# GroupNorm over a ring of six tiles: stores and loads in runs of four, last stores in quarters, one tile summed on TensorE alone

## The chip, the cores and the metric

The kernel runs on one core of one Trainium2 chip. The metric is device time in microseconds (us), as a median over executions. The kernel before takes 632.62 us (632.31 to 633.0 in the four runs beside the changed kernel). Two kernels are compared only on the same chip; runs are set side by side by their ratios to the kernel before. Each trace quoted is of a single execution.

## The reference

```python
# x: bf16 (128, 1024, 32, 16), g and b: bf16 (1024)
G = 32
xr = x.reshape(B, G, C // G, H, W)
mu = xr.mean(axis=(2, 3, 4), keepdims=True)
var = ((xr - mu) ** 2).mean(axis=(2, 3, 4), keepdims=True)
xn = ((xr - mu) / jnp.sqrt(var + 1e-5)).reshape(B, C, H, W)
return xn * g[None, :, None, None] + b[None, :, None, None]
```

A group is 32 channels of 512 elements, 16,384 in all. Four images of 32 groups fill the 128 partitions, so the work is 32 tiles of 128 x 16,384 bf16, 4.19 MB each. Each must be loaded once and stored once: 268.4 MB.

## The kernel before

A ring in SBUF, the on-chip memory, holds six tiles; a tile is normalised in place. SP, the engine that here only waits and issues, starts all large DMA transfers on one queue (the page of before: 32 loads and 35 stores, 268.44 MB, all on q1), in the order of its program, and waits for semaphores between them. In the traces the transfers land in the order of their issue.

```python
SLOTS = 6
RUNS = (2, 3, 3, 3, 3, 3, 3, 3, 3, 6)
NQ = 4
PE_CHUNKS = 12          # of 32 chunks of 512 elements; the other 20 are summed on VectorE

def store_parts(i):
    return NQ if i == NT - 1 else 1

def on_sync(e):
    def load(j):
        if j >= SLOTS:
            e.wait_ge(st[j % SLOTS], 16 * (j // SLOTS))      # the slot's store has landed
        e.dma_start(out=slot(j), in_=x_v[j]).then_inc(ld[j % SLOTS], 16)
    def store(i):
        w = F // store_parts(i)
        for p in range(store_parts(i)):
            e.wait_ge(done, NQ * i + NQ // store_parts(i) * (p + 1))   # VectorE has scaled it
            e.dma_start(...)                                            # cut
    for j in range(SLOTS):
        load(j)
    i = 0
    for run in RUNS:
        for n in range(run):
            store(i + n)
        i += run
        for j in range(i + SLOTS - run, min(i + SLOTS, NT)):
            load(j)
```

For each tile, TensorE adds 12 chunks into a PSUM buffer with an identity matrix, VectorE adds the rest in one pairing instruction, ScalarE makes the mean and then two passes of squares with the mean as bias, and VectorE scales the tile in 32 instructions.

```python
# TensorE, tile in slot c of round t
for k in range(PE_CHUNKS):
    ...                                              # waits, cut
    elif k == PE_CHUNKS - 1:
        e.wait_ge(paired, t * SLOTS + (c + 1))
    mm = e.matmul(out=sums(c), lhsT=eye[:], rhs=slot(c)[:, k * MM_FREE : (k + 1) * MM_FREE], ...)

# VectorE
pair(0)
with nc.Fori(0, NT, 1, engines=[e.engine]) as i:
    with e.If(i < NT - 1):
        e.drain()
        pair(i + 1)              # waits until TensorE has begun tile i + 1, so until it is loaded
    ...                          # wait for the deviation; scale and bias; 32 scalings; done += 1 per quarter
```

Of the kernel before, what the change touches and what calls it, by code (L numbers as in the profile page):

```python
# [14 lines left out]
EPS = 1e-5  # L15

SLOTS = 6
RUNS = (2, 3, 3, 3, 3, 3, 3, 3, 3, 6)
NQ = 4
PS_BUFS = 3  # L20
PE_CHUNKS = 12
MM_FREE = 512
# [3 lines left out]
def kernel(  # L26
# [13 lines left out]
    nc = tc.nc  # L40
# [7 lines left out]
    NT = B0 // NS  # L48
    KC = C // G
    F = KC * HW  # L50
    inv_n = 1.0 / float(F)
    NMM = F // MM_FREE
    ROUNDS = -(-NT // SLOTS)
    REST = NT - (ROUNDS - 1) * SLOTS
    KQ = KC // NQ
    PAIRED = F - PE_CHUNKS * MM_FREE
    ITEM = 2
    assert NT > SLOTS and 0 < REST < SLOTS and sum(RUNS) == NT and RUNS[-1] == SLOTS
    assert F % MM_FREE == 0 and PAIRED % 2 == 0 and SLOTS % PS_BUFS == 0
# [6 lines left out]
    def sbuf(name, shape, dtype):  # L66
        return nc.alloc_sbuf_tensor(name, shape, dtype)


    ring = sbuf("ring", [P, SLOTS * F], BF16)  # L70
# [4 lines left out]
    eye = sbuf("eye", [P, P], BF16)  # L75
# [13 lines left out]
    ps = nc.alloc_psum_tensor("ps", [P, PS_BUFS * 2 * MM_FREE], F32)  # L89
    gb_p = nc.alloc_psum_tensor("gb_p", [P, 2 * KC], F32)  # L90

    def sem(name):
        return nc.alloc_semaphore(name)
# [8 lines left out]
    first_in, paired, stded, done = (sem(n) for n in ("first", "pair", "std", "done"))  # L102
# [2 lines left out]
    )  # L105

    def store_parts(i):
        return NQ if i == NT - 1 else 1

    def slot(i):  # L110
        return ring[:, (i % SLOTS) * F : (i % SLOTS + 1) * F]

    def sums(c):
        return ps[:, c % PS_BUFS * 2 * MM_FREE : c % PS_BUFS * 2 * MM_FREE + MM_FREE]

    def sums_and_pairs(c):
        return ps[:, c % PS_BUFS * 2 * MM_FREE : c % PS_BUFS * 2 * MM_FREE + MM_FREE + 1]

    def on_sync(e):
        def load(j):  # L120
            if j >= SLOTS:
                e.wait_ge(st[j % SLOTS], 16 * (j // SLOTS))
# [5 lines that stand above are left out]
                e.wait_ge(done, NQ * i + NQ // store_parts(i) * (p + 1))  # L128
                e.dma_start(
                    out=o_v[i][:, p * w : (p + 1) * w], in_=slot(i)[:, p * w : (p + 1) * w]  # L130
                ).then_inc(st[i % SLOTS] if i + SLOTS < NT else s_fin, 16)
# [10 lines that stand above are left out]
        e.wait_ge(s_fin, 16 * sum(store_parts(i) for i in range(NT - SLOTS, NT)))  # L142
# [19 lines left out]
    def in_rounds(e, one):  # L162
        with nc.Fori(0, ROUNDS, 1, engines=[e.engine]) as t:
            for c in range(REST):
                one(c, t)
            with e.If(t < ROUNDS - 1):
                for c in range(REST, SLOTS):
                    one(c, t)

    def on_tensor(e):  # L170
        e.wait_ge(s_eye, 2)
        e.wait_ge(s_gb, 32)
        e.matmul(out=gb_p[:], lhsT=rep[:], rhs=gb_b[:], start=True, stop=True).then_inc(s_gbp, 1)  # L173

        def one(c, t):
            for k in range(PE_CHUNKS):
                if k == 0:
                    e.wait_ge(ld[c], (t + 1) * 16)
                elif k == PE_CHUNKS - 2:

                    e.wait_ge(meaned[(c - 2) % SLOTS], t + 1)
                elif k == PE_CHUNKS - 1:
                    e.wait_ge(paired, t * SLOTS + (c + 1))
                mm = e.matmul(  # L184
                    out=sums(c),
                    lhsT=eye[:],
                    rhs=slot(c)[:, k * MM_FREE : (k + 1) * MM_FREE],
                    start=(k == 0),
                    stop=(k == PE_CHUNKS - 1),
                )  # L190
                if k == 0:
                    mm.then_inc(first_in, 1)
            mm.then_inc(summed[c], 1)

        in_rounds(e, one)

    def on_scalar(e):
# [5 lines left out]
        def one(c, t):  # L203
            e.wait_ge(summed[c], t + 1)
            e.activation(  # L205
                out=jm[:], in_=sums_and_pairs(c), func=ACT.Identity, scale=-inv_n,
                accum_out=nm[:, c : c + 1], saturate=False,
            ).then_inc(meaned[c], 1)
            for h, (ready, at) in enumerate(
                ((meaned[c], t + (2 if c >= SLOTS - 2 else 1)), (half[c], t + 1))  # L210
            ):
                e.wait_ge(ready, at)
                e.activation(  # L213
                    out=ja[:],
                    in_=slot(c)[:, h * (F // 2) : (h + 1) * (F // 2)],
                    func=ACT.Square,
                    bias=nm[:, c : c + 1],
                    scale=1.0,
                    accum_out=sq[:, h : h + 1],
                    saturate=False,  # L220
                ).then_inc((half, both)[h][c], 1)
            e.wait_ge(both[c], t + 1)
            e.activation(  # L223
                out=var[:], in_=sq[:, 0:1], func=ACT.Identity, bias=eps_t[:], scale=inv_n
            ).then_inc(varred[c], 1)
            e.wait_ge(varred[c], t + 1)
            e.activation(  # L227
                out=std[:, c : c + 1], in_=sq[:, 1:2], func=ACT.Sqrt, bias=var[:], scale=inv_n
            ).then_inc(stded, 1)
# [3 lines left out]
    def on_vector(e):  # L233
        bytes_of_ring = ring[:].bitcast(mybir.dt.uint8)

        def part(i, lo, n):
            at = (i % SLOTS) * (F * ITEM) + lo * ITEM
            return bytes_of_ring[:, bass.ds(at, n * ITEM)].bitcast(BF16)

        def pair(i):  # L240
            lo, n = PE_CHUNKS * MM_FREE, PAIRED // 2
            e.wait_ge(first_in, i + 1)
            e.scalar_tensor_tensor(  # L243
                out=jp[:],
                in0=part(i, lo, n),
                scalar=1.0,
                in1=part(i, lo + n, n),
                op0=ALU.mult,
                op1=ALU.add,
                accum_out=ps[:, bass.ds((i % PS_BUFS) * (2 * MM_FREE) + MM_FREE, 1)],  # L250
                saturate=False,
            ).then_inc(paired, 1)

        e.wait_ge(s_gbp, 1)
        e.tensor_copy(out=gb[:], in_=gb_p[:])  # L255
        pair(0)
        with nc.Fori(0, NT, 1, engines=[e.engine]) as i:
            with e.If(i < NT - 1):
                e.drain()  # L259
                pair(i + 1)  # L260
            parts = [part(i, k * HW, HW) for k in range(KC)]
            e.keepalive_nop([e.lower_ap(a) for a in parts])  # L262
            e.wait_ge(stded, i + 1)
            e.reciprocal(out=rstd[:], in_=std[:, bass.ds(i % SLOTS, 1)]).then_inc(inverted, 1)  # L264
            e.wait_ge(inverted, i + 1)
            e.tensor_scalar(  # L266
                out=scl[:], in0=gb[:, 0:KC], scalar1=rstd[:], scalar2=None, op0=ALU.mult
            ).then_inc(scaled, 1)
            e.wait_ge(scaled, i + 1)
            e.scalar_tensor_tensor(  # L270
                out=bia[:], in0=scl[:], scalar=nm[:, bass.ds(i % SLOTS, 1)],
                in1=gb[:, KC : 2 * KC], op0=ALU.mult, op1=ALU.add,
            ).then_inc(shifted, 1)
            e.wait_ge(shifted, i + 1)
            for k, a in enumerate(parts):
                ts = e.tensor_scalar(  # L276
                    out=a, in0=a, scalar1=scl[:, k : k + 1], scalar2=bia[:, k : k + 1],
                    op0=ALU.mult, op1=ALU.add,
                )
                if (k + 1) % KQ == 0:  # L280
                    ts.then_inc(done, 1)

    with tc.tile_critical(no_gpsimd_drain=True):  # L283
        on_sync(nc.sync)
        on_gpsimd(nc.gpsimd)
        on_tensor(nc.tensor)
        on_scalar(nc.scalar)
        on_vector(nc.vector)
# [30 lines left out]
```

## Time and profile before

| | before |
|---|---|
| median | 632.62 us |
| profiled span | 631.1 us |
| DMA over the span | 425 GB/s, 268.44 MB |
| VectorE, ScalarE, TensorE busy | 84%, 80%, 25% |
| first packet, last landing | 2.04 us, 629.69 us |

The page cuts the span into 40 slices. These are its rows of DMA busy tenths and of bandwidth:

```profile
DMA  8999999999999999999999999999999999999996
GB/s 366 432 432 413 434 434 430 438 432 432 432 432 432 430 432 432 434 430 434 432 432 428 432 432 430 432 432 432 426 432 432 432 434 432 434 434 434 438 410 263
```

The DMA engines are busy from the second slice to the last but one. Most slices stand at 430 to 438 GB/s, and none is higher. Packets of 32 KB at 1213 ns each (below), one after another on sixteen engines, would give 432 GB/s.

The timeline of SP's DMA issues (start, time from the first issue to the last, engine, line, count):

```profile
116.30 0.33 SPq L129 DMA_DIRECT2D out_dram<-ring  x1
116.67 14.51 SPq L123 DMA_DIRECT2D ring<-in_x_dram  x3
133.53 0.34 SPq L129 DMA_DIRECT2D out_dram<-ring  x1
```

Stores 1, 3, 4 and 5 come 17.23 us apart or a multiple of it, which is the pace of VectorE in this part. So SP waits for compute before it issues those stores. The DMA queue does not mind, because loads stand between. The windows view shows that (share and GB/s are the last two columns):

```profile
core 0: us, PE busy (x) PEld busy (x) DVE busy (x) ACT busy (x) POOL busy (x), PEclk, DMA share, GB/s
125.00:130.00 5.00, 2.68 (x7) 0.67 (x5) 5.00 (x17) 5.00 (x1) 0.00 (x0) 0.73 0.99 426
130.00:135.00 5.00, 0.00 (x0) 0.00 (x0) 4.50 (x12) 4.97 (x3) 0.00 (x0) 0.61 1.02 439
135.00:140.00 5.00, 0.39 (x1) 0.10 (x1) 4.86 (x4) 3.80 (x4) 0.00 (x0) 0.50 0.99 426
```

In the timeline of VectorE, the bracket gives the idle time just before an instruction:

```profile
116.76 5.49 DVE L243 SCALAR_TENSOR_TENSOR jp<-ring 128x5120 fp8e5 x1 [0.50 <-issue]
```

More quantities come from the records of DMA packets and of semaphore updates in the same traces. The page does not print them.

- A packet of 32 KB takes 1213 ns, in loads and in stores. **Slow packet time** below is what packets take over that (over 303 ns for 8 KB), averaged over the sixteen DMA engines.
- Each transfer lands in sixteen parts (1,104 landings for the 69 transfers of before), which I take as one for each of the page's 16 DMA engines. The time from the first part to the last is the **lag** of the trailing engines. In before it is 0.6 us at the start, 0.7 us at 130 us and over 5 us at the end. Few engines make it: at 605 us five of the sixteen are 2.5 to 5.6 us behind, and the other eleven land within 0.5 us of one another.
- The **idle time** of the sixteen engines between packets is 2.2 us on average in the whole of before, and their packets take 625.0 us.

### The profile page before, as it was taken

The numbers are of one execution on the slowest core, as the hardware profiler recorded it, in microseconds if no ns is written. First come the engines' busy times: TensorE is split into PE (matmuls) and PEld (weight loads), VectorE is DVE, ScalarE is ACT, GpSimd is POOL, SyncE is SP. The second block draws the span as 40 slices with busy tenths as digits, with TensorE's granted clock in tenths as the row PEclk, the third lists the DMA queues.
The fourth block names the chain that finished last, engine by engine and source line by source line (L and its number), as shares of the span: only waits on it lengthen the run. The fifth ranks groups of instructions, "written<-read, shape, count | busy, mean of one in ns | idle before, by whom it ended". The sixth has DMA issues, their size and how long they took to land.

```text
span 631.1 us, 2973 instructions
## 1 busy us (share of the span) xinstructions
PE 158.2 (25%) x380; PEld 49.9 (8%) x385; DVE 529.4 (84%) x1185; ACT 504.0 (80%) x258; POOL 1.0 (0%) x8
## 2 busy tenths in 40 slices
PE   1523333222233330331063014203220430052000
PEld 0101111000010110110011001101000110010000
DVE  1579999999999999699689959995998699599963
ACT  0798999999999999699948977894999499859960
POOL 0000000000000000000000000000000000000000
PEclk9766555666665665666565557656665665576555
DMA  8999999999999999999999999999999999999996
GB/s 366 432 432 413 434 434 430 438 432 432 432 432 432 430 432 432 434 430 434 432 432 428 432 432 430 432 432 432 426 432 432 432 434 432 434 434 434 438 410 263
DMA packets 9744, 268.44 MB, mean 425 GB/s; under 512 B 1168, under 2 KB 1168, under 8 KB 1168
## 3 DMA queue, kind: packets, MB, share of 16 engines
q1 hardware_dynamic: 9648, 268.44, 99.0%
q10 hardware_dynamic: 96, 0.00, 0.0%
HBM read 134.22 MB, written 134.22 MB: 425 GB/s over the span
## 4 chain that ended last, share of the span: by engine, by line
ACT 50%; DMA 34%; DVE 6%; issue 5%; PE 2%; DVEq 2%; SPq 0%
ACT ja L213 46%; DMA out_dram<-ring 18%; DMA ring<-in_x_dram 16%; DVE ring L276 5%; PE ps L184 2%; ACT jm L205 2%; DVEq L259 1%; ACT var L223 1%; ACT std L227 1%; DVE jp L243 1%; DVEq L262 0%; DVEq L264 0%; DVE bia L270 0%; DVE scl L266 0%; DVEq L243 0%
## 5 line engine op out<-in xcount | busy, mean ns | idle before, releaser
L213 ACT ACTIVATE ja<-ring,nm 128x8192 fp8e5<-128x8192 bf16 x64 | 455.8, 7122 | 2.1
L276 DVE TENSOR_SCALAR ring<-ring,scl,bia x1024 | 333.5, 405 | 1.2
L184 PE MATMUL ps<-ring,eye 128*128 128x512 bf16 x379 | 158.0, 589 | 423.9 <-DVE jp L243 292.0
L243 DVE SCALAR_TENSOR_TENSOR jp<-ring 128x5120 fp8e5 (+1 forms) x32 | 175.7, 5492 | 61.4 <-PE ps L184 49.4
L205 ACT ACTIVATE jm<-ps 128x513 fp8e5<-128x513 f32 x32 | 19.3, 602 | 99.0 <-PE ps L184 99.0
L184 PEld LDWEIGHTS ps<-ring,eye 128*128 128x128 bf16 x384 | 49.8, 137 | 531.8 <-DVE jp L243 313.5
L264 DVE RECIPROCAL rstd<-std 128x1 f32 x32 | 6.3, 196 | 11.9 <-ACT std L227 11.9
L213 ACT ACTIVATION_READ_ACCUMULATOR ja<-ring,nm 128x1 f32 x64 | 11.9, 186 | 0.0
L270 DVE SCALAR_TENSOR_TENSOR bia<-scl,nm,gb 128x32 f32<-128x32 f32 x32 | 8.0, 250 | 4.2
L227 ACT ACTIVATE std<-sq,var 128x1 f32<-128x1 f32 x32 | 9.4, 295 | 1.0
L223 ACT ACTIVATE var<-sq,eps_t 128x1 f32<-128x1 f32 x32 | 9.4, 294 | 1.0
L255 DVE COPY gb<-gb_p 128x64 f32<-128x64 f32 x1 | 0.2, 225 | 11.3 <-PE gb_p L173 11.3
L266 DVE TENSOR_SCALAR scl<-gb,rstd 128x32 f32<-128x32 f32 x32 | 7.7, 241 | 1.1
L205 ACT ACTIVATION_READ_ACCUMULATOR jm<-ps 128x1 f32 x32 | 6.2, 194 | 0.0
L243 DVE DVE_READ_ACCUMULATOR jp<-ring (+1 forms) x32 | 4.5, 140 | 0.0
L173 PE MATMUL gb_p<-gb_b,rep 32*128 32x64 bf16 x1 | 0.2, 207 | 11.1 <-DMA gb_b<-in_b_dram 11.1
L201 ACT ACT_TABLE_LOAD x1 | 1.3, 1283 | 1.9 <-issue 1.9
L173 PEld LDWEIGHTS gb_p<-gb_b,rep 32*128 32x128 bf16 x1 | 0.1, 100 | 11.1 <-issue 11.1
L155 POOL TENSOR_SCALAR_AFFINE_SELECT rep<-ones_b 32x128 bf16<-32x128 bf16 x1 | 0.3, 304 | 0.0
L151 POOL TENSOR_SCALAR_AFFINE_SELECT eye<-ones_b 128x128 bf16<-128x128 bf16 x1 | 0.3, 294 | 0.4 <-issue 0.4
L201 ACT ACTIVATE warm<-eps_t 128x1 f32<-128x1 f32 x1 | 0.2, 203 | 0.0
L145 POOL MEMSET ones_b<- 128x128 bf16 x1 | 0.2, 205 | 0.5 <-SPq L283 0.5
(5 smaller groups left out, 0.5 us busy)
## 6 DMA issues: line engine op xcount, KB each, us to landing
ring<-in_x_dram SPq DMA_DIRECT2D x32, 4096.0 KB, 29.2
out_dram<-ring SPq DMA_DIRECT2D x31, 4096.0 KB, 31.5
out_dram<-ring SPq DMA_DIRECT2D x4, 1024.0 KB, 6.9
gb_b<-in_g_dram ACTq DMA_DIRECT2D x1, 2.0 KB, 6.3
gb_b<-in_b_dram ACTq DMA_DIRECT2D x1, 2.0 KB, 9.5
```

Of the source, the lines that this page charges most:

```text
L184: mm = e.matmul(out=sums(c), lhsT=eye[:], rhs=slot(c)[:, k * MM_FREE : (k + 1) * MM_FREE], start=(k == 0), stop=(k == PE_CHUNKS - 1),)
L201: e.activation(out=warm[:], in_=eps_t[:], func=ACT.Sqrt)
L205: e.activation(out=jm[:], in_=sums_and_pairs(c), func=ACT.Identity, scale=-inv_n, accum_out=nm[:, c : c + 1], saturate=False,).then_inc(me ...
L213: e.activation(out=ja[:], in_=slot(c)[:, h * (F // 2) : (h + 1) * (F // 2)], func=ACT.Square, bias=nm[:, c : c + 1], scale=1.0, accum_out= ...
L223: e.activation(out=var[:], in_=sq[:, 0:1], func=ACT.Identity, bias=eps_t[:], scale=inv_n).then_inc(varred[c], 1)
L227: e.activation(out=std[:, c : c + 1], in_=sq[:, 1:2], func=ACT.Sqrt, bias=var[:], scale=inv_n).then_inc(stded, 1)
L243: e.scalar_tensor_tensor(out=jp[:], in0=part(i, lo, n), scalar=1.0, in1=part(i, lo + n, n), op0=ALU.mult, op1=ALU.add, accum_out=ps[:, bas ...
L259: e.drain()
L264: e.reciprocal(out=rstd[:], in_=std[:, bass.ds(i % SLOTS, 1)]).then_inc(inverted, 1)
L266: e.tensor_scalar(out=scl[:], in0=gb[:, 0:KC], scalar1=rstd[:], scalar2=None, op0=ALU.mult).then_inc(scaled, 1)
L270: e.scalar_tensor_tensor(out=bia[:], in0=scl[:], scalar=nm[:, bass.ds(i % SLOTS, 1)], in1=gb[:, KC : 2 * KC], op0=ALU.mult, op1=ALU.add,). ...
L276: ts = e.tensor_scalar(out=a, in0=a, scalar1=scl[:, k : k + 1], scalar2=bia[:, k : k + 1], op0=ALU.mult, op1=ALU.add,)
```

## The change

The intent: with runs of four there are fewer changes between loading and storing. The price is that four tiles, not three, are loaded last, so the last tiles' compute comes later against the DMA. The other parts pay for that: the last three stores go out in quarters, and tile 30 is summed on TensorE alone, so that VectorE skips one pairing of 5.5 us.

```diff
-RUNS = (2, 3, 3, 3, 3, 3, 3, 3, 3, 6)
+RUNS = (2, 4, 4, 4, 4, 4, 4, 6)
@@ store_parts
-        return NQ if i == NT - 1 else 1
+        return NQ if i >= NT - 3 else 1
@@ TensorE, before the last of the 12 chunks
+                    if c == REST - 2:
+                        with e.If(t == ROUNDS - 1):
+                            with nc.Fori(PE_CHUNKS, NMM, 1, engines=[e.engine]) as more:
+                                e.matmul(out=sums(c), lhsT=eye[:],
+                                    rhs=ring[:, bass.ds(c * F + more * MM_FREE, MM_FREE)], ...)
@@ VectorE loop
-            with e.If(i < NT - 1):
+            with e.If(i == NT - 3):
+                e.memset(pairs((NT - 2) % SLOTS), 0.0).then_inc(paired, 1)
+            with e.If(i < NT - 2):
                 e.drain()
-                pair(i + 1)
+                pair(i + 1 + i // (NT - 3))
```

More of the change, by code (lines that the diff above doesn't have):

```diff
@@ L117, in sums_and_pairs, with pairs @@
         return ps[:, c % PS_BUFS * 2 * MM_FREE : c % PS_BUFS * 2 * MM_FREE + MM_FREE + 1]
+    def pairs(c):
+        return ps[:, (c % PS_BUFS * 2 + 1) * MM_FREE : (c % PS_BUFS * 2 + 1) * MM_FREE + 1]
     def on_sync(e):
@@ L182, in one @@
                 elif k == PE_CHUNKS - 1:
+                    if c == REST - 2:
+                        with e.If(t == ROUNDS - 1):
+                            with nc.Fori(PE_CHUNKS, NMM, 1, engines=[e.engine]) as more:
+                                e.matmul(
+                                    out=sums(c),
+                                    lhsT=eye[:],
+                                    rhs=ring[:, bass.ds(c * F + more * MM_FREE, MM_FREE)],
+                                    start=False,
+                                    stop=False,
+                                )
                     e.wait_ge(paired, t * SLOTS + (c + 1))
```

## The prediction

> **What bounds it now.** DMA. The page's row of slices shows the 16 DMA engines 90% busy or more in all slices but the first and last, at 426 to 438 GB/s in most. [...] DVE is busy 84%, ACT 80%. In the timeline compute takes 17.23 us a tile where DVE is saturated (pairing 5.49 us, 32 scalings 10.42 us); DMA needs 19.4 us for a tile's load and store, 9.7 us each. Packets of 32 KB take 1213 ns, loads and stores alike. Averaged over the DMA engines, packets fill 624 us and gaps 2.7 us. Some DMA engines trail the others (spread of each transfer's sixteen landings), by 0.7 us at 130 us and 5 us at the end; about 0.12 us comes with each store, less with the changes from loads to stores.
>
> **What the change does.**
> 1. Two changes from loads to stores fewer. There some packets take 0.1 to 0.9 us longer, but the trailing engine loses only some 0.2 us each. Estimated gain 0.4 us.
> 2. SP issues in order, and loads stand behind stores that wait for compute. In the first run of four, store 5 goes ahead of load 8. In before's timeline stores 1 to 5 are issued at compute's pace: 64.6, 82.6, 99.1, 116.3, 133.5 us. Store 4 landed at 130.2 (first engine) to 130.8 us (last), so its data ended near 130. Before, load 8, queued at 116.7 us, covered this; after, the queue runs dry until store 5 is issued at 133.5 us, and its first packet comes 1 us later (as at the start: issue 1.02, packet 2.04 us). [...] Loss: 4 to 5 us, never recovered, since all that follows is DMA-bound. No later run stalls: store 9 should be ready near 207 us and wanted near 212; later runs have over 5 us of slack.
> 3. At the end four tiles are loaded last instead of three, so compute is 7.5 us (17.2 - 9.7) later against DMA. The TensorE sum takes 5.5 us of pairing off DVE, and quarters let stores 29 and 30 start up to 7.8 us earlier. By my reckoning the last quarter is ready within 1 us of when the leading DMA engines want it; the trailing ones do not notice. So these parts pay for the longer run and gain nothing. Four 8 KB packets take 4 x 309 = 1236 ns against 1213: 0.4 us more for two tiles.
>
> Sum: +4.5 - 0.4 + 0.4, about +4.5 us on 632.6.
>
> **Predicted: 637.0 us, 80% range 634.0 to 640.5.** Faster by over 2%: 1%. Within 2%: 97%. Slower: 2%.
>
> **What would show it.** A DMA dip between 128 and 137 us; store 5 issued at 133.5 us as before, loads 8 and on behind it; DMA busy elsewhere; gaps up by about 5 us, busy time unchanged within 1 us; the lag at the end 4 to 5 us; DVE no longer pairing tile 30, TensorE running 32 products for it.
>
> **What would make it wrong.** Direction changes costing more than the packets show; a second dry queue at 207 to 212 us if DVE's added branch or later loads slow the chain (3 us more); a TensorE loop slower than 0.43 us a product, so that the last tile is over 5 us late; the trailing engines catching up in the gap and not falling back.

## More of the kernel before

Store 4 is issued at 116.30 us; three loads follow; store 5 comes at 133.53 us.

## The result, and the profile after

The changed kernel takes 639.90 us (639.85 to 640.33) against 632.62 us, a ratio of 1.0116 with a 95% interval of 1.0099 to 1.0134. It is slower by 7.3 us: within 2%, but clear of noise. A ratio is the mean time of one kernel's runs over that of the other's of the same rounds, so it is not quite the ratio of the medians.

The page's rows of slices, after:

```profile
DMA  8999999969999999999999999999999999999996
GB/s 362 431 440 411 431 435 433 435 269 394 427 425 429 427 427 435 435 438 431 429 427 435 435 440 429 427 431 435 433 438 429 427 431 438 431 438 427 421 427 279
```

There is one hole, in the ninth slice (about 128 to 144 us), where 269 GB/s stands in place of 432. The tenth slice is low too, at 394. The windows view of after, with two windows from further on:

```profile
125.00:130.00 5.00, 4.08 (x11) 1.26 (x9) 5.00 (x17) 4.97 (x3) 0.00 (x0) 0.64 0.84 360
130.00:135.00 5.00, 0.00 (x0) 0.00 (x0) 5.00 (x17) 4.97 (x3) 0.00 (x0) 0.71 0.00 0
135.00:140.00 5.00, 0.00 (x0) 0.00 (x0) 4.21 (x2) 4.97 (x3) 0.00 (x0) 0.50 0.99 419
...
620.00:625.00 5.00, 0.00 (x0) 0.00 (x0) 4.29 (x15) 0.34 (x2) 0.00 (x0) 0.50 0.59 247
625.00:630.00 5.00, 0.00 (x0) 0.00 (x0) 5.00 (x17) 0.00 (x0) 0.00 (x0) 0.50 0.98 400
```

From 130 to 135 us nothing moves, while VectorE and ScalarE are fully busy. (The share seems to count a packet wholly in the window where it starts, since some windows exceed 1, so 0.99 in the next window includes some idle time.) The packet records put the idle time of the DMA engines at 6.3 us between 125 and 140 us; I call this the hole. (The expectations below, written earlier, say 6.1 us.) SP's timeline says why:

```profile
117.70 0.33 SPq L132 DMA_DIRECT2D out_dram<-ring  x1
...
135.23 0.33 SPq L132 DMA_DIRECT2D out_dram<-ring  x1
135.61 12.08 SPq L126 DMA_DIRECT2D ring<-in_x_dram  x4
```

Nothing is issued between store 4 at 117.70 us and store 5 at 135.23 us. Load 8, whose slot had been free since store 2 landed at about 111 us, stands behind store 5 in SP's program. Store 5 comes 1.70 us later than before did it, though its compute is the same. The timeline of VectorE shows the cause:

```profile
118.46 5.49 DVE L256 SCALAR_TENSOR_TENSOR jp<-ring 128x5120 fp8e5 x1 [0.79 <-issue]
```

The gap ahead of the pairing is 0.79 us where it was 0.50 us. Six such turns precede the end of tile 5: 6 x 0.29 = 1.7 us.

Two things in the edit could cost this: the added branch, and the index `i + 1 + i // (NT - 3)` in place of `i + 1`. The same traces hold the records of VectorE's sequencer, the part that runs branches and register arithmetic (the page leaves them out), and they part the two. The sequencer runs ahead of the scalings and then waits in the `drain` until they are done (in after from 114.42 to 117.72 us, while the scalings last until 117.67 us). The added compare-and-branch comes before that wait: it takes 0.21 us, and the drain is shorter by as much (3.29 us against 3.50), so it costs nothing here. After the drain come three register instructions that work out what the pairing waits for and its addresses. From the end of the drain to the pairing they take 0.74 us (178, 265 and 138 ns, and the gaps between them), where before they took 0.45 us (40, 130 and 115 ns). So the 0.29 us is the index arithmetic, not the branch. On VectorE this trace has 84 ns from the start of a compare-and-branch to the next instruction where the body of the `If` follows, and 206 ns (median) for the added one, which in all turns but one skips its body.

The end has a smaller hole, at 620 to 625 us. The timelines of VectorE's last 32 scalings, of before and then of after:

```profile
610.14 10.42 DVE L276 TENSOR_SCALAR ring<-ring,scl,bia  x32
```

```profile
621.37 10.42 DVE L293 TENSOR_SCALAR ring<-ring,scl,bia  x32
```

In before the last quarter is scaled at 620.6 us, and the last landing is at 629.69 us, 9 us later, because the trailing DMA engines are still busy with older work (the sixteen parts of the last store land from 624.78 to 629.69 us). After, it is scaled at 631.8 us and the last landing is at 636.38 us, 4.6 us later: the DMA engines have been waiting for compute (2.1 us of idle time from 620 to 625 us, against 0.3 us in before). ScalarE sets that pace. The timeline of after shows its square passes of the last two tiles with hardly a gap:

```profile
589.53 7.12 ACT L226 ACTIVATE ja<-ring,nm 128x8192 fp8e5<-128x8192 bf16 x1
...
596.78 7.12 ACT L226 ACTIVATE ja<-ring,nm 128x8192 fp8e5<-128x8192 bf16 x1
...
605.26 7.12 ACT L226 ACTIVATE ja<-ring,nm 128x8192 fp8e5<-128x8192 bf16 x1
...
612.51 7.12 ACT L226 ACTIVATE ja<-ring,nm 128x8192 fp8e5<-128x8192 bf16 x1
```

The end of the last packet moved from 629.24 to 635.93 us, by 6.7 us. Averaged over the sixteen DMA engines that is 5.1 us more idle time (2.2 to 7.3) and 1.6 us more packet time (625.0 to 626.6).

### The profile page after: what moved, and what is told of

It reads as the page before. It is cut to its first block, busy times and chain, and to the rows that moved or that the text cites. A ratio compares the mean times of both kernels' runs of the same rounds, so it can differ in the third digit from the quotient of the medians.

```text
span 638.1 us, 3113 instructions
## 1 busy us (share of the span) xinstructions
PE 158.4 (25%) x400; PEld 51.2 (8%) x405; DVE 524.2 (82%) x1184; ACT 504.0 (79%) x258; POOL 1.0 (0%) x8
## 4 chain that ended last, share of the span: by engine, by line
ACT 49%; DMA 25%; DVE 12%; issue 8%; DVEq 3%; PE 2%; another core or an unknown queue 1%; SPq 0%; ACTq 0%
ACT ja L226 45%; DMA ring<-in_x_dram 25%; DVE ring L293 10%; PE ps L197 2%; ACT jm L218 2%; DVEq L276 1%; ACT var L236 1%; ACT std L240 1%; DVE jp L256 1%; DVEq L279 0%; DVEq L256 0%; SPq L132 0%; DVE bia L287 0%; DVE scl L283 0%
## 5 line engine op out<-in xcount | busy, mean ns | idle before, releaser
L197 PE MATMUL ps<-ring,eye 128*128 128x512 bf16 x379 | 152.7, 577 | 420.6 <-DVE jp L256 265.3
L256 DVE SCALAR_TENSOR_TENSOR jp<-ring 128x5120 fp8e5 (+1 forms) x31 | 170.3, 5493 | 75.5 <-PE ps L197 58.1
L197 PEld LDWEIGHTS ps<-ring,eye 128*128 128x128 bf16 x384 | 49.2, 135 | 523.6 <-DVE jp L256 310.2
L189 PE MATMUL ps<-ring,eye 128*128 x20 | 5.7, 382 | 0.8
L189 PEld LDWEIGHTS ps<-ring,eye 128*128 128x128 bf16 x20 | 1.9, 97 | 4.6 <-issue 3.2
```

The source lines that it names most:

```text
L189: e.matmul(out=sums(c), lhsT=eye[:], rhs=ring[:, bass.ds(c * F + more * MM_FREE, MM_FREE)], start=False, stop=False,)
L256: e.scalar_tensor_tensor(out=jp[:], in0=part(i, lo, n), scalar=1.0, in1=part(i, lo + n, n), op0=ALU.mult, op1=ALU.add, accum_out=ps[:, bas ...
```

## The experiments

**Theory.** The DMA queue runs dry once, because load 8 stands behind a store that waits for compute; the changed VectorE loop makes that longer; a small rest is lost at the end. **Rivals.** Each run of four costs something; or the tail parts (quarters, TensorE sum) cost the time. Where the expectations speak of the branch in VectorE's loop, they mean all that was added there; that its cost is the index arithmetic was read from the traces only afterwards.

All eleven kernels gave correct results, and each was timed in five rounds against before.

### runs_only: the run lengths alone

```diff
 # before
-RUNS = (2, 3, 3, 3, 3, 3, 3, 3, 3, 6)
+RUNS = (2, 4, 4, 4, 4, 4, 4, 6)
```

> The kernel before with the new run lengths alone: no quarters for stores 29 and 30, no TensorE-only sum, the VectorE loop as it was. Theory (one dry DMA queue in the first run of four, made longer by the VectorE branch of the changed kernel): store 5 issued at 133.5 us, DMA idle near 4.4 us between 125 and 140 us (6.1 in the changed kernel), no other idle time before 590 us; then a compute-bound end, so about 640.4 us (ratio near 1.012). Rival (each run of four costs the same): idle or late landings in every one of the six runs, and a time near the changed kernel's with no dip of its own at 130 us. Second rival (the tail parts cost the time): under 635 us.

Measured: 640.30 us, ratio 1.0123 (1.0108 to 1.0139). The hole was 4.7 us, with nothing over 0.12 us in any 5 us stretch from there until 610 us, and then 6.0 us from 610 to 620 us. The new run lengths alone cause the loss. In net the tail parts gain next to nothing (1.0116 with them).

### tail_only: the tail parts alone

```diff
 # the changed kernel
-RUNS = (2, 4, 4, 4, 4, 4, 4, 6)
+RUNS = (2, 3, 3, 3, 3, 3, 3, 3, 3, 6)
```

> The changed kernel with the old run lengths (2, eight of 3, 6): quarters and the TensorE-only sum alone. Theory: no dry queue, though stores 2 to 5 come 0.3 us a tile later because of the branch; 633.0 us (ratio 1.000 to 1.002). Rival (tail parts cost the time): 637 us or more.

Measured: 633.59 us against 632.62 us, ratio 1.0017 (1.0003 to 1.003). No hole at 130 us. The second rival falls: the tail parts cost about 1 us, not seven.

### late_fours: fours only where compute is ahead

```diff
 # the changed kernel
-RUNS = (2, 4, 4, 4, 4, 4, 4, 6)
+RUNS = (2, 3, 3, 3, 3, 4, 4, 4, 6)
```

> The changed kernel with runs 2, four of 3, three of 4, 6: the fours come only when compute is ahead. Theory: no idle DMA near 130 us or in any later run of four; what is left against before is the tail, about 634 us (ratio 1.000 to 1.004). Rival (each run of four costs the same, about 1.2 us each): half of the loss stays, about 636.2 us.

Measured: 634.87 us, ratio 1.0040 (1.0027 to 1.0054). No hole before 615 us, where 2.3 us are idle in the compute-bound end. Ratio and time are nearer the theory than the rival's 636.2 us, if not by much; the next experiment is sharper.

### after_peeled: the added branch and index arithmetic taken out of the loop

```diff
 # the changed kernel, VectorE; scale(i) is the rest of the loop's body
-        with nc.Fori(0, NT, 1, engines=[e.engine]) as i:
-            with e.If(i == NT - 3):
-                e.memset(pairs((NT - 2) % SLOTS), 0.0).then_inc(paired, 1)
-            with e.If(i < NT - 2):
+        with nc.Fori(0, NT - 3, 1, engines=[e.engine]) as i:
+            with e.If(i < NT - 1):
                 e.drain()
-                pair(i + 1 + i // (NT - 3))
-            ...
+                pair(i + 1)
+            scale(i)
+        e.memset(pairs((NT - 2) % SLOTS), 0.0).then_inc(paired, 1)
+        e.drain()
+        pair(NT - 1)
+        for i in range(NT - 3, NT):
+            scale(i)
```

> The changed kernel with the last three tiles of the VectorE loop written out, so that the loop has one branch again as in before; same work, same order. Theory: idle before each pairing 0.50 us instead of 0.79, store 5 issued at 133.5 us instead of 135.2, dip near 4.4 us instead of 6.1, time 639.9 - 1.7 - 0.3 = about 637.9 us (ratio 1.0085). Rival (the branch does not matter, the dip has another cause): 639.9 us as the changed kernel.

Measured: 638.41 us, ratio 1.0095 (1.0079 to 1.011), against 1.0116 with the changed loop. The hole shrank from 6.3 to 4.8 us, and VectorE's line has its old gap:

```profile
116.82 5.49 DVE L256 SCALAR_TENSOR_TENSOR jp<-ring 128x5120 fp8e5 x1 [0.49 <-issue]
```

Store 5 was issued just before 134 us. Some 1.3 to 1.5 us of the loss comes with the changed loop (the intervals of the two ratios overlap; the times, at most 638.50 us against at least 639.85, do not). The edit removes the branch and the longer index together, so the time does not part them. The sequencer's records do: no branch is left inside this loop, the drain is 3.57 us long, longer even than before's 3.50, and from its end to the pairing it is 0.45 us, as in before.

### one_load_ahead: one load moved ahead of one store

```diff
 # the changed kernel, SP
             for n in range(run):
+                if i + n == 5:
+                    load(8)
                 store(i + n)
             i += run
             for j in range(i + SLOTS - run, min(i + SLOTS, NT)):
-                load(j)
+                if j != 8:
+                    load(j)
```

> The changed kernel with one load moved: SP issues load 8 ahead of store 5; nothing else differs, every run of four and all tail parts stay. Theory (the DMA queue runs dry because load 8 stands behind store 5): the dip at 130 to 136 us is gone (idle under 0.3 us), all later landings come about 6 us earlier, 634.3 us (ratio near 1.003). Rival (a cost of runs of four as such, or of the tail): 639 us or more.

Measured: 634.82 us against 632.85 us, ratio 1.0040 (1.0027 to 1.0054). SP's timeline and the windows view of this kernel:

```profile
117.55 0.33 SPq L132 DMA_DIRECT2D out_dram<-ring  x1
117.92 0.46 SPq L126 DMA_DIRECT2D ring<-in_x_dram  x1
...
135.08 0.33 SPq L132 DMA_DIRECT2D out_dram<-ring  x1
```

```profile
125.00:130.00 5.00, 3.12 (x10) 1.00 (x8) 5.00 (x17) 4.97 (x3) 0.00 (x0) 0.81 0.99 426
130.00:135.00 5.00, 0.00 (x0) 0.00 (x0) 5.00 (x16) 4.97 (x3) 0.00 (x0) 0.53 1.03 446
135.00:140.00 5.00, 0.00 (x0) 0.00 (x0) 4.21 (x2) 4.97 (x3) 0.00 (x0) 0.50 0.97 406
```

Store 5 still waits for compute until 135 us, but load 8 is in the queue and the hole is gone. Moving one instruction took away two thirds of the loss (1.0116 to 1.0040), with all six runs of four in place. This shows the cause of the hole: the order on SP, not the length of the runs as such.

### first_four: one early run of four, all else as before

```diff
 # before
-RUNS = (2, 3, 3, 3, 3, 3, 3, 3, 3, 6)
+RUNS = (2, 4, 2, 3, 3, 3, 3, 3, 3, 6)
```

> The kernel before with runs 2, 4, 2, six of 3, 6: a single run of four, at the early place. Theory: one dip near 4.5 us at 130 us and no other idle time, then DMA-bound to the end as before, with the trailing engines' lag smaller by some 0.5 us: 636.6 us (ratio near 1.0063), over half of the loss of the whole change. Rival (each run of four costs the same): about 633.8 us.

Measured: 638.23 us against 632.85 us, ratio 1.0087 (1.0074 to 1.0101). The direction was right, and the rival of equal cost for each run fell, but my number was 1.6 us too low. The hole was 4.9 us, so something else cost time. Slow packet time shows it:

| stretch | before | first_four | after | one_load_ahead |
|---|---|---|---|---|
| 55 to 65 us | 0.8 us | 0.6 us | 0.7 us | 0.8 us |
| 130 to 145 us | 0.0 us | 0.95 us | 0.8 us | 0.2 us |
| 145 to 240 us | 0.2 us | 0.9 us | 1.0 us | 0.3 us |
| 138 to 150 us | 0.0 us | 0.9 us | 0.9 us | 0.15 us |
| 178 to 192 us | 0.0 us | 0.8 us | 0.85 us | 0.0 us |

In first_four and in after nearly all slow packets beyond 130 us fall in the last two stretches. These hold the next change from a store to loads and the next from loads to stores. After the hole all DMA engines start together, and the sixteen parts of a transfer land within 0.7 us of one another. The first change of every kernel, at 60 us, has engines as close (0.6 us in before), and costs nearly as much. This gave a new theory: **a dry queue costs its length and then slows the next two changes of direction, because the DMA engines are in step.**

The next run tests the first half of it. The reason given in the second half does not fit the records. In before, the change at 130 us has a lag of 0.7 us and no slow packets. In first_four the lag stays at 0.3 to 0.7 us through the five changes between 190 and 320 us, and these have 0.1 us of slow packets together. And one_load_ahead, without any hole, has 0.8 us at 405 to 415 us and again at 560 to 570 us, with lags of 3.1 to 3.5 us. So being in step, as the landings measure it, is neither enough nor needed, and why the two changes after a hole are slow stays open.

### dip_late: a hole made on purpose, in mid-run

```diff
 # before, SP, in store(i)
+            if i == 14:
+                e.wait_ge(done, NQ * 17 + 1)
             for p in range(store_parts(i)):
```

> The kernel before with one extra wait on SP: store 14 waits until a quarter of tile 17 is scaled, so that the DMA queue runs dry once in mid-run (leading engines done near 335 us, trailing near 336.5; store 14 near 344.5, first packet near 345.5). This measures what a dry queue costs beyond its length. Theory formed from first_four (a dry queue puts the DMA engines in step, and the next two changes of direction then cost all sixteen 0.8 us each): idle near 10 us, landings of all engines within 0.5 us of one another after it, packets longer by some 0.8 us at each of the next two changes, and a time of 632.8 + 9 + 1.5 - 0.5 (lag not regained) = about 642.8 us (ratio 1.016). Rival (a dry queue costs its length, less what the trailing engines catch up): 632.8 + 10 - 1.5 = about 641.0 us or less, packets after it no longer than in before.

Measured: 643.43 us against 632.53 us, ratio 1.0173 (1.0159 to 1.0186). The idle time was 12 us on average, more than I had expected. The lag was 3.6 us before the hole (one engine; the other fifteen within 1.0 us) and 0.2 us after it. The windows view of dip_late at the next two changes of direction, with the window before the first:

```profile
365.00:370.00 5.00, 0.00 (x0) 0.00 (x0) 4.65 (x15) 4.97 (x3) 0.00 (x0) 0.50 1.16 498
370.00:375.00 5.00, 0.00 (x0) 0.00 (x0) 0.00 (x0) 4.93 (x4) 0.00 (x0) 0.50 0.93 341
...
400.00:405.00 5.00, 0.00 (x0) 0.00 (x0) 4.50 (x13) 4.97 (x3) 0.00 (x0) 0.74 0.99 341
```

The same windows of before:

```profile
365.00:370.00 5.00, 0.00 (x0) 0.00 (x0) 4.24 (x14) 4.97 (x3) 0.00 (x0) 0.50 0.97 419
370.00:375.00 5.00, 0.00 (x0) 0.00 (x0) 0.00 (x0) 4.53 (x4) 0.00 (x0) 0.50 0.99 426
...
400.00:405.00 5.00, 4.47 (x11) 1.51 (x10) 4.83 (x17) 4.56 (x3) 0.00 (x0) 0.58 0.99 426
```

The engines are busy in both kernels. The fall from 426 to 341 GB/s overstates what was lost, since a packet counts where it starts: the window before has 498, and the stretch from 365 to 375 us has 419 against 423. With each packet's bytes spread over its duration, the packet records give 389 and 366 GB/s in the two windows, against 433 and 432. Slow packet time, which does not depend on windows, was 0.9 us at the first change and 1.0 us at the second, and 0.0 us in both places in before. So the pattern of first_four, two slow changes after a hole, was foretold and found at another place, and all seven runs with such a hole show it (0.7 to 1.0 us at each of the two). Its reason is not shown by any run.

### no_pe_sum and no_quarters: the tail parts one by one

```diff
 # no_pe_sum: before, with
+RUNS = (2, 4, 4, 4, 4, 4, 4, 6)
+        return NQ if i >= NT - 3 else 1
 # no_quarters: the changed kernel, with
+        return NQ if i == NT - 1 else 1
```

> The kernel before with the new run lengths and the quarters for stores 29 and 30, without the TensorE-only sum. Theory: dip near 4.6 us at 130 us as in runs_only; the end is set by the compute of tile 31, which quarters of earlier tiles do not move, so the time is that of runs_only to within 0.5 us: 640.1 us (ratio near 1.012), last scaling done near 633 us. Rival (the quarters are what shortens the end): 638.5 us or less.

> The changed kernel with only the last store in quarters, as before; the TensorE-only sum stays. Theory: dip of 6.1 us as in the changed kernel, last scaling done at 631.8 us as there, but store 30, issued whole near 616 us, holds the DMA until 627 us, so the quarters of tile 31 end about 1 us later: 640.9 us (ratio near 1.013). Rival (the 8 KB packets of the quarters cost time): 639.4 us or less.

Measured: no_pe_sum 640.12 us, ratio 1.0117 (1.0102 to 1.0133), the hole 4.9 us, last scaling done at 632.7 us. no_quarters 641.09 us, ratio 1.0135 (1.0119 to 1.015), the hole 6.3 us, last scaling done at 631.6 us. Both came out as expected. The quarters are worth about 1.2 us at the end of the changed kernel (1.0135 to 1.0116). The TensorE sum is worth nothing as written: it shortens the end, but the index arithmetic that came with it lengthens the hole. after_peeled shows the sum without that (1.0095 to 1.0117 without the sum: 1.4 us). In both comparisons the intervals overlap while the times do not (640.87 us or more against 640.33 or less; 638.50 or less against 640.12 or more), so the signs are safer than the sizes.

### twos and mid_fours: is there anything to gain from run lengths?

```diff
 # before, twos
+RUNS = (2,) * 13 + (6,)
 # before, mid_fours
+RUNS = (2, 3, 3, 4, 4, 4, 3, 3, 6)
```

> The kernel before with runs of 2 throughout (thirteen of 2, then 6): 13 changes from stores to loads where before has 9. If the changes of direction cost time, as the intent of the change has it, some 1 to 3 us more: 634 to 636 us. Theory (with the DMA engines out of step a change costs next to nothing on the average engine): 632.3 to 633.5 us, no dry queue.

> The kernel before with runs 2, 3, 3, 4, 4, 4, 3, 3, 6: three runs of four where compute is ahead, three loads last, none of the tail parts: the candidate to beat both. If fewer changes of direction gain: 631.5 us. Theory: no dry queue, nothing gained, 632.3 to 633.3 us (ratio 1.000).

Measured: twos 632.92 us, ratio 1.0010 (0.9997 to 1.0024); mid_fours 632.43 us, ratio 1.0002 (0.9988 to 1.0015), both against 632.53 us. (The expectation for twos counts before's changes as 9 without the last one.) Neither differs from before. While the queue stays full, four changes of direction more cost nothing that could be measured, and one fewer gained nothing. So no version that beats both kernels was found; mid_fours, the candidate, only equals the better one.

## Why the prediction was right, and where it was off

The time was predicted as 637.0 us with a range of 634.0 to 640.5; it is 639.9 us, 0.6 us inside the upper end. The cause was foreseen; that the number still fell within the range owes something to luck, since everything that was missed made the kernel slower.

1. *Fewer changes of direction gain 0.4 us.* No gain is to be seen: twos and mid_fours have 1.0010 and 1.0002. The conclusion that this part of the intent had nothing to win was right. The reason was incomplete. Changes were cheap in before (0.2 us of slow packets from 145 to 240 us) and, by their times, in twos and mid_fours, but each of the two after a hole had 0.8 to 1.0 us of slow packets, averaged over the sixteen engines, and some later ones in one_load_ahead had 0.8 us without a hole.
2. *Store 5 goes ahead of load 8 and the queue runs dry.* Right in place, cause and sign. one_load_ahead takes the hole away by moving that one load, and first_four makes it with a single run of four. The term was mis-sized: 4 to 5 us predicted, a hole of 6.3 us measured, and nearly 0.9 us of slow packets at each of the next two changes on top. Store 5 was to be issued at 133.5 us as before; it was issued at 135.23. So 1.5 us of the hole is what was added to the VectorE loop. I had listed the added branch there as a danger for a later store (store 9) but not counted it for store 5, and it was the index arithmetic beside it that cost the time. The slow packets I had not foreseen; "busy time unchanged within 1 us" failed, with 1.6 us more, of which I estimate about 0.4 us for the quarters (in place of 256 packets of 32 KB at 1213 ns there are 1,024 of 8 KB at 309 ns, the median: 5.9 us over sixteen engines).
3. *No later run stalls.* Right: no 5 us stretch between 140 and 600 us of after has over 0.12 us of idle time.
4. *The tail parts pay for the fourth tile and gain nothing.* Nearly. They do not quite pay: with the early hole gone, late_fours and one_load_ahead both stay at 1.0040, 2 us above before, and show 1.2 to 2.3 us of idle time at 615 to 620 us. I reckoned that the trailing engines would not notice. But compute of a tile here waits for the last of its sixteen parts, so a lag of 3 us at the load of tile 28 (544.9 to 548.0 us; one engine, the other fifteen within 0.8 us) held back the start of the last chain: TensorE begins that tile at 548.05 us. What this cost in the end no run shows. Of the 2 us, about 1 us comes with the tail parts themselves (tail_only, 1.0017); I did not part the rest further.
5. *The lag at the end is 4 to 5 us.* It was under 1 us at the last landing, since compute had become the last to finish, and 3.6 us before the last tiles.

As a sum: the early hole with what follows from it is worth 1.0116 - 1.0040, or 4.8 us of the 7.3 us. The remaining 2 to 2.5 us is what one_load_ahead and late_fours still lose, with compute last to finish and with more packet time than before (627.7 and 626.6 us against 625.0); I did not part it. The 4.8 us is less than hole plus slow packets (6.3 + 1.7). Part of the difference is that one_load_ahead has slow packets of its own later (6.0 us of slow packet time in all, against 4.9 in after). It also has no hole, across which the lag fell from 3.6 to 0.2 us in dip_late; what that is worth in time no run shows.

## What to carry to other kernels

Where all transfers go through one in-order queue of a DMA-bound kernel, ask of each store that waits for compute what is already queued behind the DMA engines at that moment, and place a load that is free to go ahead of it. In these runs longer runs were safe only once compute was ahead (mid_fours 1.0002; late_fours without a hole before 615 us); during the fill, where stores come at the pace of compute (17.23 us), one run too long cost its hole (4.9 us in first_four), and the slow changes of direction after it (0.8 and 0.9 us of slow packets). Index arithmetic in a compute engine's loop can lengthen such a hole in every turn (0.29 us here), while a branch that falls in a wait of the sequencer cost nothing (0.21 us, with the drain shorter by as much): before blaming an instruction, look whether it stands before or after the wait.
